# Chunked attention with a gated convolution on one core: the first half pair in two halves, fp32 value products at the start, three more half pairs with row sums on ScalarE, a new order

## The chip, the cores and the metric

The kernel runs on one core of one Trainium2 chip. Its engines are TensorE (PE; its weight loads are listed as PEld), VectorE (DVE), ScalarE (ACT), GpSimd (POOL) and SyncE (SP), which issues the DMAs. Each works off its own instructions in order. The metric is the time of the program on the device in microseconds; less is better.

## The reference

```
scores = q_c @ k_c^T / 8            # chunks of 64 rows, head size 64
attn   = exp(scores - max); attn = attn / (sum(attn) + 1e-9)
x      = attn @ v_c, heads side by side            # [8, 576, 512]
gate   = sigmoid(sum over 5 taps of conv_w[k] * x shifted by 4-k rows)
out    = (gate * (x @ w_val)) @ w_out
```

q, k and v are [8 batches, 8 heads, 576 rows, 64], all float32. The two weight matrices and the taps reach the device in 64-bit floats and are turned into float32 there.

## The kernel before, in words

The 4608 rows are cut into 9 groups g of 512 rows; the 512 columns into 4 blocks of 128. A group's attention runs in two half pairs p = 0, 1 of four heads each, which give column blocks 0, 1 and 2, 3 of x. All work is written as small pieces, and the text ORDER lists the pieces one after another; each engine gets its instructions in that order and never passes one. SLOTS says which buffer each new tile takes.

The pieces of one half pair (g, p): `lq`, `lk`, `lv` load 512 KB each. `S g p b` makes the scores of one half b (16 small fp32 matmuls) in the tile `s`, of which there is one for all half pairs. `mx` takes the row maxima (DVE), `sb` subtracts them into an `e_row` buffer (DVE), `ex` is the exponential (ACT), `sm` the row sums and their reciprocals (DVE), `nm` the division (POOL, `nmD` on DVE). For four half pairs `ng`, `ea`, `rc` stand in for `sb`, `ex`, `sm`: ACT reads the scores out of `s`, adds the negative maximum, and adds up each row as it goes, in 16 instructions. Half pair (0, 1) subtracts its maxima by four matmuls (`mh`, `mlD`, `sp`, `ep`). `T` transposes the result (8 matmuls into tile `et`), `ec` copies it (ACT), `A` multiplies by the values into two `ps` tiles (32 small matmuls). `xc` copies these into x; `xr` and `xd` split x into a rounded part and a rest for the value product.

The pieces of one group: `hl` is the halo of x, `k0` and `k g c 1..4` the five taps of block c (DVE but for `k0`), `sg` the sigmoid (ACT). `V g m c` is the value product, block c into output block m: three matmuls with w_hi x_hi, w_lo x_hi and w_hi x_lo, so that rounded operands reach nearly fp32. `vc` (ACT) or `vcD` (DVE) copies its result, `gs` (DVE) or `gsG` (POOL) multiplies it by the gate, `gr` (ACT) rounds, `gd` (POOL) or `gdD` (DVE) takes the rest. `P g t c` is the output product, three matmuls again; `oc` or `ocD` copies it and `st` stores it.

The weights: `lw` loads a block, `w1` to `w5`, `w7` turn it into float32 bits (`wq`), `w6` and `wb` split them into `v_hi`, `v_lo` (or `o_hi`, `o_lo`). `W n` issues n matmuls on a tile of zeros whose result is not used. `ps` has four tiles, all of 128x512.

In the profile nearly every row says L160 (L162 in the changed kernel), the line of the helper that records all pieces, so pieces are told apart by tiles. The tiles named t2 and t4 and a digit are shared homes; the views write most of them as t.

Of the kernel before, what the change touches and what calls it, by code (L numbers as in the profile page):

```python
# [8 lines left out]
F32 = mybir.dt.float32  # L9
# [11 lines left out]
T 0 0,ep 0 1,w4 v 0,ec 0 0,sm 0 1,w7G v 0,S 1 0 0,S 1 0 1,A 0 0,lv 0 1,w6 v 0,mx 1 0,nm 0 1,lk 2 0,lc,W 2,xr 0 0 0,
lv 1 0,sb 1 0,xc 0 0 1,xr 0 0 1,wb v 0,T 0 1,xd 0 0 0,ex 1 0,xd 0 0 1,S 1 1 0,w1G v 3,ec 0 1,S 1 1 1,sm 1 0,w7G v 1,
V 0 3 0,lq 2 1,w5 v 3,lw o 0,w2 v 3,mx 1 1,A 0 1,lk 2 1,nm 1 0,xc 0 0 0,lw o 1,lw o 3,V 0 2 0,sb 1 1,xr 0 1 0,lk 3 0,
w6 v 1,T 1 0,xr 0 1 1,w3 v 3,wbD v 1,xc 0 1 0,S 2 0 0,xc 0 1 1,w4 v 3,S 2 0 1,w6 v 2,xd 0 1 0,w7G v 3,ec 1 0,V 0 3 1,
# [12 lines left out]
V 2 1 0,w4 o 1,sg 0 1,V 2 0 3,k 1 2 1,w6 o 3,k0 2 0,V 2 1 1,gdD 0 0,vc 2 0,w7 o 1,V 2 3 2,gr 0 3,k 1 0 2,V 2 1 2,
k0 1 1,k 1 2 2,V 2 2 0,gr 0 2,gdD 0 3,w6 o 1,V 2 1 3,w3 o 2,w2 o 2,ng 4 0,P 0 1 0,gs 0 1,vc 2 1,k 1 2 3,V 2 2 1,gr 0 1,
wbD o 1,V 2 3 3,gdD 0 1,V 2 2 2,w4 o 2,ex 3 1,P 0 2 0,k 1 3 1,V 2 2 3,vc 2 3,w7 o 2,T 3 0,gdD 0 2,w6 o 2,sm 3 1,vc 2 2,
P 0 1 1,wb o 2,ea 4 0,P 0 3 0,wbD o 3,P 0 0 0,k 1 1 1,P 0 0 1,nmD 3 1,P 0 1 2,P 0 1 3,k 1 3 2,P 0 0 2,k 1 1 2,P 0 0 3,  # L40
ec 3 0,k 1 0 3,P 0 2 1,k 1 1 3,oc 0 1,P 0 3 1,k 1 0 4,k0 2 1,P 0 2 2,oc 0 0,k0D 2 2,k 1 1 4,T 3 1,k 2 2 1,P 0 3 2,
# [530 lines left out]
```

## Time and profile before

| what | value |
|---|---|
| three runs | 284.43, 286.24, 287.78 us (median 286.24) |
| span of the profiled execution, first to last instruction | 286.4 us |
| busy PE, DVE, ACT, POOL | 274.4, 245.8, 198.1, 105.2 us |
| mean granted clock of TensorE | 0.994 |
| moved by DMA | 42.47 MB |

The profiled execution is not timed apart from its span, which lies 0.2 us above the median of the three runs; the runs spread by 3.3 us. A busy time counts an engine's own instructions; PE's includes the warm-up matmuls `W`. Instructions of one engine overlap at their ends, so the distance between two starts, not the length of one, says how fast a queue moves.

### The profile page before, as it was taken

The numbers are of one execution on the slowest core, as the hardware profiler recorded it, in microseconds if no ns is written. First come the engines' busy times: TensorE is split into PE (matmuls) and PEld (weight loads), VectorE is DVE, ScalarE is ACT, GpSimd is POOL, SyncE is SP. The second block draws the span as 40 slices with busy tenths as digits, with TensorE's granted clock in tenths as the row PEclk, the third lists the DMA queues.
The fourth block names the chain that finished last, engine by engine and source line by source line (L and its number), as shares of the span: only waits on it lengthen the run. The fifth ranks groups of instructions, "written<-read, shape, count | busy, mean of one in ns | idle before, by whom it ended". The sixth has DMA issues, their size and how long they took to land.

```text
span 286.4 us, 7971 instructions
## 1 busy us (share of the span) xinstructions
PE 274.4 (96%) x3344; PEld 217.3 (76%) x3347; DVE 245.8 (86%) x357; ACT 198.1 (69%) x451; POOL 105.2 (37%) x93
## 2 busy tenths in 40 slices
PE   7978899999999999999999999989999999999994
PEld 3456688878888887878787888767678778888883
DVE  0899779999999999999999999999999899974210
ACT  2479588898999979964898696788586742751101
POOL 1457775273013506551874003976400400013100
PEclk9999799999999999999999999999999999999999
DMA  7999964457002605666250256441100121021245
GB/s 280 416 391 359 380 239 130 169 181 260 3 2 78 222 0 185 221 223 211 86 185 2 73 201 218 173 144 44 39 0 1 39 89 61 0 100 49 110 171 195
DMA packets 14291, 42.47 MB, mean 148 GB/s; under 512 B 1712, under 2 KB 1712, under 8 KB 14256
## 3 DMA queue, kind: packets, MB, share of 16 engines
q1 hardware_dynamic: 14256, 41.97, 40.9%
q8 instruction: 26, 0.43, 0.6%
q14 instruction: 9, 0.07, 0.1%
HBM read 32.53 MB, written 9.44 MB: 147 GB/s over the span
## 4 chain that ended last, share of the span: by engine, by line
PE 69%; DVE 19%; DMA 3%; issue 3%; POOL 2%; ACT 2%; SPq 0%; POOLq 0%
PE ps L160 61%; DVE acc L160 8%; PE s L160 5%; DVE t L160 4%; PE et L160 4%; DVE rs L160 3%; DMA ld<-in_v 2%; DMA ld<-in_q 1%; POOL acc L160 1%; POOL t L160 1%; DVE mx L160 1%; ACT x L160 1%; DVE t2o L160 1%; DVE t4a L160 0%; DVE x L160 0%
## 5 line engine op out<-in xcount | busy, mean ns | idle before, releaser
L160 DVE SCALAR_TENSOR_TENSOR acc<-x,cw,acc 128x516 f32<-128x516 f32 (+1 forms) x144 | 105.1, 771 | 0.9 <-POOL acc L160 0.6
L160 PE MATMUL ps<-t,v_hi 128*128 128x512 f32 x240 | 85.3, 402 | 0.0
L160 PE MATMUL ps<-t,v_lo 128*128 128x512 f32 x136 | 53.9, 396 | 0.0
L160 PEld LDWEIGHTS ps<-t,v_hi 128*128 128x128 f32 x240 | 45.2, 188 | 11.0 <-issue 0.5
L160 PE MATMUL ps<-o_hi,t 128*128 128x512 f32 x120 | 46.4, 403 | 0.8 <-ACT x L160 0.7
L160 PE MATMUL ps<-o_lo,t 128*128 128x512 f32 x76 | 30.0, 395 | 0.0
L160 DVE TENSOR_REDUCE mx<-s 128x16 f32<-128x1024 f32 x18 | 21.8, 1211 | 9.3 <-PE s L160 9.2
L160 PEld LDWEIGHTS ps<-t,v_lo 128*128 128x128 f32 x136 | 25.7, 189 | 5.1
L160 PEld LDWEIGHTS ps<-o_hi,t 128*128 128x128 f32 x120 | 22.5, 188 | 7.3 <-ACT x L160 1.1
L160 POOL TENSOR_TENSOR t<-e_row,rs 128x1024 f32<-128x1024 f32 x13 | 26.4, 2033 | 4.2 <-DVE rs L160 3.4
L160 PEld LDWEIGHTS s<-ld,ld 64*64 64x64 f32 x1152 | 19.4, 139 | 9.6 <-issue 7.7
L160 ACT CAST t<-ps 128x512 fp32r<-128x512 f32 x34 | 19.4, 596 | 10.0 <-PE ps L160 8.1
L160 PE MATMUL s<-ld,ld 64*64 64x64 f32 x1152 | 22.0, 227 | 2.9 <-issue 1.9
L160 ACT ACTIVATE e_row<-s,mx 128x64 f32<-128x64 f32 x64 | 19.0, 352 | 4.7 <-DVE mx L160 4.7
L160 POOL COPY x<-x 128x16 f32<-128x16 f32 x8 | 2.8, 354 | 52.6 <-DVE acc L160 44.9
L160 PEld LDWEIGHTS ps<-t,ld 64*64 64x64 f32 x960 | 16.3, 140 | 5.0 <-issue 2.1
L160 PE MATMUL ps<-t,ld 64*64 64x64 f32 x960 | 18.1, 225 | 1.9 <-DVE t2i L160 1.1
L160 POOL TENSOR_SCALAR acc<-x,cw 128x516 f32<-128x516 f32 (+1 forms) x7 | 12.7, 1820 | 19.2 <-ACT x L160 7.4
L160 ACT ACTIVATE acc<-x,cw 128x516 f32<-128x516 f32 (+1 forms) x24 | 17.6, 740 | 1.9 <-DVE x L160 1.8
L160 ACT ACT_TABLE_LOAD x14 | 18.0, 1283 | 0.9 <-PEq L561 0.7
L160 DVE TENSOR_REDUCE rs<-e_row 128x16 f32<-128x1040 f32 x14 | 17.2, 1228 | 1.6 <-ACT e_row L160 1.6
L160 ACT COPY x<-ps 128x512 f32<-128x512 f32 (+3 forms) x38 | 16.0, 476 | 3.3 <-issue 2.0
(302 smaller groups left out, 572.5 us busy)
## 6 DMA issues: line engine op xcount, KB each, us to landing
ld<-in_k SPq DMA_DIRECT2D x18, 512.0 KB, 5.8
ld<-in_q SPq DMA_DIRECT2D x18, 512.0 KB, 5.9
ld<-in_v SPq DMA_DIRECT2D x18, 512.0 KB, 5.0
out<-t SPq DMA_DIRECT2D x10, 256.0 KB, 2.3
acc<-in_moe_w_val SPq DMA_DIRECT2D x4, 512.0 KB, 7.5
acc<-in_moe_w_out SPq DMA_DIRECT2D x4, 512.0 KB, 7.1
out<-t2j SPq DMA_DIRECT2D x3, 256.0 KB, 2.5
out<-t2b SPq DMA_DIRECT2D x3, 256.0 KB, 3.1
```

Of the source, the lines that this page charges most:

```text
L160: return tc.keep_in_program_order(fn(*args, **kwargs))
```

## The change

Half pair (0, 0) is loaded, scored, normalised, transposed and multiplied in two halves. Its half b = 1 has its scores in the bank of `et`. Its x is no longer split: a new piece `F 0 m c` multiplies x blocks 0 and 1 as fp32 by the unsplit weights `wq`, one fp32 matmul for the three of `V`, eight pieces in all; `xr` and `xd` of (0, 0) are gone. `ea` becomes four pieces `ey g p 0..3` of four rows each, which may stand apart, and the half pairs (1, 1), (2, 1) and (4, 1) join (3, 0), (4, 0), (7, 0) and (8, 0) in that form. All `ocD` become `oc`. `gs` on DVE falls from 18 to 4 and `gsG` rises from 14 to 28; `gdD` falls from 21 to 12 and `gd` rises from 15 to 24. The warm-up matmuls fall from 31 (8, 15, 6, 2) to 21 (1, 6, 1, 1, 1, 8, 1, 1, 1). ORDER and SLOTS are written anew.

```diff
-ORDER = """zw,lk 0 0,zi,lq 0 0,W 8,lw v 2,lw v 0,lq 0 1,zr 1,zm,lk 0 1,lw v 1,zr 0,lv 0 0,lq 1 0,S 0 0 0,S 0 0 1,W 15,mx 0 0,
...
+ORDER = """zw,zi,zr 0,zr 1,lk 0 0 0,lq 0 0 0,lk 0 0 1,zm,W 1,lq 0 0 1,S 0 0 1,mx 0 0 1,sb 0 0 1,lw v 3,ex 0 0 1,w1G v 3,S 0 0 0,
+mx 0 0 0,W 6,lw v 0,lq 0 1,w3 v 0,W 1,sb 0 0 0,sm 0 0 1,lk 0 1,S 0 1 0,S 0 1 1,w2G v 3,w3 v 3,w5 v 0,ex 0 0 0,sm 0 0 0,
...
-BY_HALF = set()
+BY_HALF = {(0, 0)}
...
-        if b == 0:
-            s_ps[g, p] = tile_of("s", [P, 2, 2, 4, D], F32, banks)
-        at = s_ps[g, p]
-        if b == 1 and (g, p) in BY_HALF:
-            at = s_ps[g, p, 1] = tile_of("et", [P, 2, 2, 4, D], F32, banks)
+        alone = (g, p) in BY_HALF
+        if b == 0 or alone:
+            s_ps[g, p, b] = tile_of("et" if b else "s", [P, 2, 2, 4, D], F32, banks)
+        at = s_ps[g, p, b if alone else 0]
...
-    def sm(g, p):
-
-        rss[g, p] = r = tile_of("rs", [P, 16], F32)
-        run(V.tensor_reduce, out=r, in_=probs[g, p], op=ALU.add, axis=AX.X)
+    def sm(g, p, b=None):
+
+        if (g, p) not in rss:
+            rss[g, p] = tile_of("rs", [P, 16], F32)
+        r, e = rss[g, p], probs[g, p]
+        if b is not None:
+            r, e = r.rearrange("p (h b c) -> p h b c", h=2, b=2)[:, :, b], half_rows(e, b)
...
+    def ey(g, p, i):
+
+        if (g, p) not in probs:
+            probs[g, p] = e_rows[next(e_slot)]
+            rss[g, p] = tile_of("rs", [P, 16], F32)
+        h, b = i // 2, i % 2
+        at = half_scores(g, p, b)
+        for c in range(4):
+            j = 4 * i + c
+            run(S.activation, out=probs[g, p][:, j, 0:D], in_=at[:, h, c], func=AF.Exp, bias=mxs[g, p][:, j:j + 1],
+                scale=SCALE, accum_out=rss[g, p][:, j:j + 1])
+
     def ea(g, p):
-
-        probs[g, p] = e_rows[next(e_slot)]
-        rss[g, p] = r = tile_of("rs", [P, 16], F32)
-        sb, m = flat(s_ps[g, p]), mxs[g, p]
-        for j in range(16):
-            run(S.activation, out=probs[g, p][:, j, 0:D], in_=sb[:, j], func=AF.Exp, bias=m[:, j:j + 1], scale=SCALE,
-                accum_out=r[:, j:j + 1])
-
-    def rc(g, p):
...
-    def nm(g, p, on=G):
-        normed[g, p] = tile_of("en", [P, 16, D], F32)
-        run(on.tensor_tensor, out=normed[g, p], in0=probs[g, p][:, :, 0:D], in1=wide(rss[g, p]), op=ALU.mult)
+    def nm(g, p, *half):
+        *b, on = half if half and not isinstance(half[-1], int) else (*half, G)
+        if (g, p) not in normed:
+            normed[g, p] = tile_of("en", [P, 16, D], F32)
+        out, e, r = normed[g, p], probs[g, p][:, :, 0:D], wide(rss[g, p])
+        if b:
+            out, e = half_rows(out, *b), half_rows(e, *b)
+            r = rss[g, p].rearrange("p (h b c) -> p h b c", h=2, b=2)[:, :, b[0]].unsqueeze(3).broadcast_to([P, 2, 4, D])
+        run(on.tensor_tensor, out=out, in0=e, in1=r, op=ALU.mult)
...
+    def tr(g, p, b=None):
+        if (g, p) not in et_ps:
+            et_ps[g, p] = tile_of("et", [P, 8, P], F32, banks)
         for j in range(8):
-            run(E.transpose, out=et_ps[g, p][:, j, :], in_=normed[g, p][:, 2 * j:2 * j + 2, :].rearrange("p b k -> p (b k)"), identity=ident)
-
-    def ec(g, p, copy=S.copy):
-
...
+    def av(g, p, only=None):
         et, vv = probs_t[g, p], vt[g, p]
         for u in range(2):
-            x_ps[g, p, u] = tile_of("ps", [P, 2, 2, 2, D], F32, banks)
-        for b in range(2):
+            if (g, p, u) not in x_ps:
+                x_ps[g, p, u] = tile_of("ps", [P, 2, 2, 2, D], F32, banks)
...
+    def vf(g, m, c):
+        if c == 0:
+            v_ps[g, m] = tile_of("ps", [P, T], F32, banks)
+        run(E.matmul, v_ps[g, m], lhsT=wq["v", c].bitcast(F32)[:, m * P:(m + 1) * P], rhs=xs[g][:, c, begin(g):],
+            start=c == 0, stop=c == NH - 1)
```

PE, from the transposes of half pair (0, 1) to the first value products; first the kernel before, then the changed one (`et` are transposes, `s` scores, `ps` the value product):

```order
L160 MATMUL et_356<-ident,t_339 128x128 x8
L160 MATMUL s_369<-ld_161,ld_226 64x64 x32
L160 MATMUL ps_410<-t_348,v_hi 128x512
L160 MATMUL ps_410<-t_348,v_lo 128x512
L160 MATMUL ps_410<-t4a,v_hi 128x512
```

```order
L162 MATMUL s_319<-ld_291,ld_293 64x64 x32
L162 MATMUL et_355<-ident,t_309 128x128 x8
L162 MATMUL ps_371<-x_246,t_141 128x512
L162 MATMUL ps_371<-x_246,t2a 128x512
L162 MATMUL ps_382<-x_246,t_141 128x512
```

Before, scores of half pair (1, 1) and products of split x (three for each block) follow; now the scores come first and the products read x itself, one for each block, from two unsplit weight tiles.

ACT, from the last weight block of `v` to the first work on half pair (1, 1) in the changed kernel, and the same stretch of the kernel before (`mx` is the row maximum, `acc` on the right a raw weight):

```order
L160 CAST v_hi<-t_486 128x512
L160 ACTIVATE cw_r<-raw_cw 128x20
L160 ACTIVATE cw_t<-cw_t 128x20
L160 ACTIVATE e_row_65<-e_row_65 128x16x64
L160 ACTIVATE t_596<-acc_418 128x512
L160 CAST t_601<-ps_550 128x2x256
L160 ACTIVATE e_row_64<-e_row_64 128x16x64
L160 COPY t_621<-ps_466 128x512
```

```order
L162 CAST t_424<-ps_390 128x2x256
L162 ACTIVATE acc_437<-x_246,cw 128x512
L162 ACTIVATE acc_445<-x_246,cw 128x512
L162 ACTIVATE t2f<-acc_364 128x512
L162 ACTIVATE e_row_65,rs_486<-s_450,mx_483 128x64 x16
L162 COPY t_555<-et_529 128x1024
L162 COPY t2i<-ps_504 128x512
L162 ACTIVATE t2j<-acc_598 128x512
```

Before, two whole exponentials over `e_row` stand here; now 16 exponentials that read `s` itself stand in one piece, behind two taps and a weight step and ahead of the copy of the next transpose.

DVE, around the row maxima of half pair (7, 1), before and then changed:

```order
L160 TENSOR_REDUCE mx_2673<-s_2600 128x16
L160 SCALAR_TENSOR_TENSOR acc_2315<-x_2127,cw,acc_2315 128x516
L160 TENSOR_TENSOR t2p<-t2o,t2i 128x512
L160 TENSOR_TENSOR t_2706<-ps_2635,t_2697 128x2x256
L160 COPY x_2564<-ps_2635 128x2x256
L160 SCALAR_TENSOR_TENSOR acc_2338<-x_2127,cw,acc_2338 128x516
L160 TENSOR_TENSOR t_2706<-ps_2636,t_2697 128x2x256
L160 TENSOR_TENSOR e_row_64<-s_2600,mx_2673 128x16x64
L160 TENSOR_TENSOR t2k<-t_2633,t2j 128x512
```

```order
L162 TENSOR_TENSOR t_2572<-ps_2516,t_2550 128x2x256
L162 TENSOR_REDUCE mx_2604<-s_2482 128x16
L162 TENSOR_TENSOR e_row_65<-s_2482,mx_2604 128x16x64
L162 SCALAR_TENSOR_TENSOR acc_2243<-x_2201,cw,acc_2243 128x516 x2
L162 TENSOR_TENSOR t_2664<-ps_2615,t4a 128x2x256
L162 SCALAR_TENSOR_TENSOR acc_2380<-x_2201,cw,acc_2380 128x516
L162 TENSOR_TENSOR t_2664<-ps_2614,t4a 128x2x256
L162 SCALAR_TENSOR_TENSOR acc_2380<-x_2201,cw,acc_2380 128x516
L162 SCALAR_TENSOR_TENSOR acc_2691<-x_2587,cw,acc_2691 128x516
```

The gate product (t2p) and the rest (t2k) that stood between the taps and the splits are no longer on DVE here.

## Rows read from the trace of the kernel before

**Rows 1.** The start in stretches, and two stretches later on, by window (columns as headed).

```profile
core 0: us, PE busy (x) PEld busy (x) DVE busy (x) ACT busy (x) POOL busy (x), PEclk, DMA share, GB/s
0.00:10.00 10.00, 7.90 (x78) 3.83 (x80) 2.72 (x4) 2.85 (x4) 2.12 (x11) 1.00 0.83 318
10.00:20.00 10.00, 9.09 (x219) 5.98 (x220) 9.11 (x15) 6.24 (x10) 4.06 (x4) 1.00 1.03 410
20.00:30.00 10.00, 7.34 (x189) 5.45 (x192) 9.41 (x15) 9.47 (x16) 7.87 (x7) 1.00 0.99 362
180.00:190.00 10.00, 8.99 (x100) 7.10 (x98) 9.33 (x11) 6.59 (x10) 9.25 (x9) 1.00 0.25 95
200.00:210.00 10.00, 9.33 (x60) 7.33 (x51) 9.97 (x16) 5.01 (x16) 3.96 (x3) 1.00 0.08 28
```

**Rows 2.** Waits of PE, longest in total first.

```profile
PE s L160 <- issue: 1.9, 1, 1.9
...
PE ps L160 <- DVE t2i L160: 1.1, 1, 1.1
PE ps L160 <- DMA ld<-in_v: 0.8, 1, 0.8
```

**Rows 3.** The granted clock (PEclk) in two windows, columns as in group 1.

```profile
28.00:30.00 2.00, 0.24 (x14) 0.24 (x18) 1.58 (x5) 1.82 (x3) 1.80 (x2) 1.00 1.03 401
31.00:35.00 4.00, 4.00 (x71) 3.03 (x70) 3.96 (x7) 1.06 (x3) 2.25 (x2) 0.57 1.01 367
```

**Rows 4.** Timeline of PE from 0 to 13 us.

```profile
1.17 3.59 PE L160 MATMUL ps<-warm 128*128 128x512 bf16 x8 [1.17 <-DVE warm L160]
5.47 1.99 PE L160 MATMUL s<-ld,ld 64*64 64x64 f32 x64 [0.71 <-DMA ld<-in_q]
...
8.22 4.14 PE L160 MATMUL ps<-warm 128*128 128x512 bf16 x13 [0.22 <-issue]
```

**Rows 5.** Page, costliest groups of PE, the warm-up matmuls.

```profile
L160 PE MATMUL ps<-warm 128*128 128x512 bf16 x28 | 10.1, 509 | 1.6 <-DVE warm L160 1.2 <-issue 0.4
```

**Rows 6.** Timeline at the end of the span.

```profile
282.39 0.39 PE L160 MATMUL ps<-o_hi,t2h 128*128 128x512 f32 x1
282.82 0.58 ACT L160 COPY t<-ps 128x512 f32<-128x512 f32 x1 [0.76 <-PE ps L160]
```

**Rows 7.** Timeline of PE, value product, score and transpose.

```profile
50.24 0.40 PE L160 MATMUL ps<-t4b,v_hi 128*128 128x512 f32 x1
50.47 0.40 PE L160 MATMUL ps<-t,v_hi 128*128 128x512 f32 x1
...
58.24 1.16 PE L160 MATMUL s<-ld,ld 64*64 64x64 f32 x64
...
60.27 1.09 PE L160 MATMUL et<-ident,t 128*128 128x128 f32 x8
```

**Rows 8.** Timeline of the first half pairs, three engines.

```profile
7.52 1.23 DVE L160 TENSOR_REDUCE mx<-s 128x16 f32<-128x1024 f32 x1 [6.41 <-PE s L160]
...
17.57 1.01 ACT L160 COPY t4b<-et 128x1024 f32<-128x1024 f32 x1 [0.34 <-PE et L160]
...
19.11 1.90 POOL L160 TENSOR_TENSOR t<-e_row,rs 128x1024 f32<-128x1024 f32 x1
```

**Rows 9.** Timeline of ACT, copies and the first row-sum exponential.

```profile
47.34 0.59 ACT L160 COPY t2j<-ps 128x512 f32<-128x512 f32 x1
47.82 0.61 ACT L160 CAST t<-ps 128x512 fp32r<-128x512 f32 x1
...
51.81 0.32 ACT L160 ACTIVATE e_row<-s,mx 128x64 f32<-128x64 f32 x1 [0.93 <-DVE mx L160]
...
56.57 0.67 ACT L160 COPY t2i<-ps 128x512 f32<-128x512 f32 x1
```

**Rows 10.** Timeline of DVE and POOL side by side.

```profile
184.38 1.29 POOL L160 TENSOR_TENSOR t<-t,t 128x512 f32<-128x512 f32 x1
...
184.44 1.78 DVE L160 SCALAR_TENSOR_TENSOR acc<-x,cw,acc 128x516 f32<-128x516 f32 x1 [0.64 <-POOL acc L160]
```

More of the change, by code (lines that the diff above doesn't have):

```diff
@@ L37 @@
[L37 to L41, printed above, removed]
@@ L293, in mx @@
         if b is None:
-            run(V.tensor_reduce, out=mxs[g, p], in_=flat(s_ps[g, p]), op=ALU.max, axis=AX.X)
+            run(V.tensor_reduce, out=mxs[g, p], in_=flat(s_ps[g, p, 0]), op=ALU.max, axis=AX.X)
         else:
@@ L302, in sb @@
         if b is None:
-            run(V.tensor_tensor, out=e, in0=flat(s_ps[g, p]), in1=wide(mxs[g, p]), op=ALU.subtract)
+            run(V.tensor_tensor, out=e, in0=flat(s_ps[g, p, 0]), in1=wide(mxs[g, p]), op=ALU.subtract)
         else:
@@ L353, in rc @@
-    def rc(g, p):
+    def ey(g, p, i):
[8 more added lines that the diff above has]
+                scale=SCALE, accum_out=rss[g, p][:, j:j + 1])
+    def ea(g, p):
+        for i in range(4):
+            ey(g, p, i)
@@ L367, in ec @@
-    def ec(g, p, copy=S.copy):
-        probs_t[g, p] = tile_of("eb", [P, 2, 2, 2, P], F32)
-        run(copy, out=probs_t[g, p].rearrange("p h b a q -> p (h b a) q"), in_=et_ps[g, p])
-    def av(g, p):
+    def nm(g, p, *half):
[7 more added lines that the diff above has]
+        run(on.tensor_tensor, out=out, in0=e, in1=r, op=ALU.mult)
@@ new lines, in tr, with ec @@
+    def tr(g, p, b=None):
+        if (g, p) not in et_ps:
+            et_ps[g, p] = tile_of("et", [P, 8, P], F32, banks)
+        for j in range(8):
+            if b is not None and j // 2 % 2 != b:
+                continue
+            at = j if b is None else 4 * b + 2 * (j // 4) + j % 2
+            run(E.transpose, out=et_ps[g, p][:, at, :], in_=normed[g, p][:, 2 * j:2 * j + 2, :].rearrange("p b k -> p (b k)"), identity=ident)
+    def ec(g, p, *half):
+        *b, copy = half if half and not isinstance(half[-1], int) else (*half, S.copy)
+        if (g, p) not in probs_t:
+            probs_t[g, p] = tile_of("eb", [P, 2, 2, 2, P], F32)
+        if b:
+            run(copy, out=probs_t[g, p][:, :, b[0]],
+                in_=et_ps[g, p][:, 4 * b[0]:4 * b[0] + 4].rearrange("p (h a) q -> p h a q", h=2))
+        else:
+            run(copy, out=probs_t[g, p].rearrange("p h b a q -> p (h b a) q"), in_=et_ps[g, p])
@@ L373, in av @@
+    def av(g, p, only=None):
         et, vv = probs_t[g, p], vt[g, p]
         for u in range(2):
-            x_ps[g, p, u] = tile_of("ps", [P, 2, 2, 2, D], F32, banks)
-        for b in range(2):
+            if (g, p, u) not in x_ps:
+                x_ps[g, p, u] = tile_of("ps", [P, 2, 2, 2, D], F32, banks)
+        for b in range(2) if only is None else [only]:
             for a in range(2):
@@ L399, in xc @@
             if lo < hi:
-                run(copy, out=xs[g][:, 2 * p:2 * p + 2, col + lo - t:col + hi - t],
+                run(copy, out=x_of(g)[:, 2 * p:2 * p + 2, col + lo - t:col + hi - t],
                     in_=x_ps[g, p, u].rearrange("p b a w t -> p b (a w t)")[:, :, lo - u * half:hi - u * half])
@@ L406, in xr @@
     def xr(g, p, u):
-        if u == 0:
+        if (g, p) not in xh:
             xh[g, p] = tile_of("xh", [P, 2, T], F32R)
```

202 lines of the change are left out of this document (107 added, 95 removed).

## Prediction

> **What bounds the kernel now.** I read the windows first. After the first 30 us PE is busy nearly without a break; in the first 30 us it is busy for 7.90, 9.09 and 7.34 of each 10 us [rows 1], so 5.7 us are idle. A busy share says nothing of what the work is, so I looked at what PE does there: the warm-up matmuls, whose result nobody uses, take 10.1 us by their group [rows 5]. Next the clock: from 31 to 35 us it is granted at 0.57 of full speed, most of it at the lower of the two levels (1.2 and 2.4 GHz), behind a stretch in which PE was busy for 0.24 of 2 us [rows 3]; four microseconds at 0.57 give away 1.7 us. The first score pair takes 1.99 us and a later one 1.16 [rows 4, 7], another 0.8 us. Then the waits of PE behind the start: 0.8 us for a load of v, 1.1 us for a DVE copy, and 0.7 us in the window from 200 us, in which DVE is busy for 9.97 of 10 [rows 1, 2]. Last the end: the last matmul starts at 282.39 us, ACT copies its result from 282.82 us, and the store ends the span at 286.4, so 3.6 us lie behind PE [rows 6]. Together 5.7 + 10.1 + 1.7 + 0.8 + 2.6 + 3.6 = 24.5 us are not work of PE, and 261.9 us are. PE is the bound; what can be won is those 24.5 us, above all the 18.3 at the start. DVE is the second bound from 40 us on and makes the later waits.
>
> **The change, part by part.** I price by starts, since instructions of one engine overlap at their ends. A matmul of 128x512 takes 0.23 us (50.24 to 50.47) [rows 7], so `V` takes 0.70. A score pair takes 1.1 us, a transpose 0.9 to 1.1 [rows 7].
>
> *The fp32 product.* The trace has no fp32 matmul of 512 columns. From below, two passes at the pace of a rounded matmul are 0.47 us; from above, eight transposes of 128 fp32 columns in 1.09 us are 1.06 ns a column and, with two passes, 1.09 us for 512. I take 0.87, from the transposes at 0.85 ns a column without the tail of the last one, as scores and transposes are the nearest fp32 rows. Against 0.70 for the three matmuls of `V` the eight pieces cost 8 x 0.17 = 1.4 us more on PE (1.8 us less to 3.1 us more). The work becomes 263.3 us. The Trainium skill (FP8 and Floating Point Precision, TensorE Precision Notes) says that true fp32 takes four passes through the array; four times 0.23 us would be 0.92, and the sum would rise by 0.4 us. No run shows such a matmul yet.
>
> *What leaves the other engines.* `xr` and `xd` of (0, 0) go, and the first product needs neither `v_hi` nor `v_lo`. Three half pairs lose `sb` and `sm` on DVE, and 11 `ocD`, 14 `gs`, 9 `gdD` go to ACT and POOL: some 3 x 2.6 + 2 x 0.6 + 11 x 0.6 + 23 x 0.7, about 32 us less on DVE, where an instruction of 512 takes 0.6 to 0.7 and one of 1024 takes 1.23 [rows 8]. ACT gains 3 x 4.76 us for the row sums (51.81 to 56.57 for 16 rows of four pieces) and 11 copies of 0.5 us (47.34 to 47.82), and loses three exponentials of 1 us, two roundings and three weight steps, which leaves about 15 us more [rows 9]. POOL gains 23 products of 1.3 us, about 30 us [rows 10]. With 198 us on ACT and 105 on POOL before, neither becomes the bound over the whole span. So it is decided in the first 110 us, where all three follow PE closely.
>
> *The start.* I walked the new order of the four engines with the durations of the rows. Loads land as now: data comes in at 318 GB/s in the first 10 us, 410 in the next, 362 in the third [rows 1], so a load of 512 KB takes 1.3 us. The four half loads land at 5.4 us, the fifth and sixth load (second half pair) at 11.0, v at 14.9, q of (1, 0) at 17.4, q of (1, 1) at 24.2. Half b = 1 is scored to 6.4 us, the other half to 7.4. The DVE passes over half a tile take 0.65 us, half of 1.23 [rows 8], and sum up to both reciprocals at 10.3 and 11.5 us; here a weight step waits for its load at 8.5 us with both `sb` and `sm` queued behind it. POOL divides in two passes of 1.05 us, half of 1.9 to 2.0 [rows 8], behind two weight steps, to 14.2 us; the transposes end at 14.7, against a copy of the whole transpose at 17.57 now [rows 8]. ACT copies the two halves at 15.3 and 17.2 us, as the exponential of (0, 1) stands between them; the second half of `A` ends at 17.8. ACT then has weight steps queued between the two copies of x, which end at 19.2 and 20.8. PE meanwhile does S (1, 0) and the transposes of (0, 1), to 20.9, and begins the fp32 products then. Three of those, `A` of (0, 1), the fourth, S (1, 1), two more, five `V` and a transpose follow. ACT reaches the new row sums of (1, 1) at 28.95 us, when the maximum is ready, and ends them at 33.7. The next scores (2, 0) need the one tile `s` and so that end; PE is through with the work ahead of them at 33.8. The cover is exact, and each microsecond that ACT loses earlier comes out on PE.
>
> By 33.8 us PE will have done 4.4 us of scores, 2.75 of transposes, 2.2 of `A`, 0.9 of maxima, 5.2 of fp32 products, 3.5 of `V`: 18.95. So 14.9 us are lost at the start, against 18.3 now.
>
> *The sum.* Work 263.3, lost at the start 14.9, end 3.6. A walk of this kind leaves out handing over between engines (0.05 to 0.1 us each) and a clock that falls: 1.0 us. Later waits: DVE's share falls, but up to 110 us ACT is nearly as full as PE; 1.0 us instead of 2.6. That gives **283.8 us**, 0.9% under 286.24. I take the profile's span as the time before.
>
> **The rivals.** *A cold start.* The order has one warm-up matmul ahead of the first scores instead of eight, then seven, not fifteen. Now the eight take 3.59 us, 0.45 each, twice the warm pace, and the first scores are slow too; only late among the next thirteen (4.14 us) does the pace reach 0.2 [rows 4]. The changed order has idle stretches before and behind the second scores. If PE stays at the lower level up to the first products, the steps of the walk on its path grow: second scores 1.1 us, maxima 0.9, eight warm-up matmuls 1.7, `A` 1.1. Those are 4.8 us, all ahead of ACT's copies of x and so of the row sums on which (2, 0) waits: 288.6, slower than now. It decides from 2.4 us on; below that the kernel stays ahead. Against it: the scores and seven matmuls from 5.4 to 10.4 us are as dense a stretch as the one behind which the pace rose now.
>
> *Loads set the start.* DMA moves 362 to 410 GB/s from 10 to 30 us [rows 1] and PE waits 1.9 us at a score whose load is late [rows 2]. Half loads in rows of 2 KB, or a later fifth load, of 2 us would move every step by 2 us: 285.8.
>
> *POOL holds DVE up.* A tap (two inputs from SBUF) that starts beside a POOL product takes 1.78 us instead of 0.7 and ends with it [rows 10]. The Trainium skill (GPSIMD Engine Reference, Specifications) says that POOL's SBUF interfaces are shared with VectorE, with contention where DVE has two SBUF inputs; by that rule, which this row agrees with, all 23 moved products would speak against the change. Counted in the order up to `P 2`, only some 5 of them lie in the first 110 us, where DVE follows closely; with 1.1 us each, and half of it hidden, that is 2.7 us: 286.5. Behind that the same count leaves DVE 10 to 40 us behind PE's work.
>
> *Nothing of what I added happens.* Without the two allowances and with fp32 products at 0.75 us it is 283.8 - 2.0 - 1.0 = 280.8.
>
> **How the numbers follow.** Forecast (282.3 to 285.3) 0.36, cold start 0.14, loads 0.16, POOL 0.10, all allowances unneeded 0.24. A measurement of this kernel tells about 1% from no change: under 283.4 is faster, over 289.1 slower. Half of the forecast's case and nearly all of the last one are faster: 0.43. Slower is the cold case's upper part, with the fp32 product at its upper bound: 0.12. The rest, 0.45, is the same. The range reaches from the last case, 280.3, to between POOL's and the cold case, 287.8, and leaves out 2 in 10.
>
> **What the profile will show.** Right: fp32 products of two matmuls each from about 21 us, at 0.87 us a piece; scores (2, 0) at about 34 us, released by ACT; 15 us of PE lost before; DVE near 215 us busy, ACT near 214; no PE waits of over 0.5 us behind 110 us. Wrong: a lower granted clock or 0.43 us per matmul behind 11 us (cold start); PE or DVE waiting for loads of q or k (loads); taps of over 1.2 us in number between 40 and 110 us (POOL); the row sums of (1, 1) begun much later than 29 us, which would make the start worth nothing.

## The result, and the profile after

The changed kernel takes 288.96 us (median of four runs, 288.70 to 289.96); the kernel before, beside it, takes 287.01 (four runs, 284.43 to 290.70). The ratio is 1.0107, interval 1.0059 to 1.0155: about 1% slower, where 0.9% faster was forecast. The ratio is over fast runs alone, so without the 290.70, which lies over 1.5% above the fastest run of the same kernel. A second series of the same kernel gave 288.85 us and 1.0078 (1.0047 to 1.0109).

The profiled execution was the longest of its four runs, 289.96 us with a span of 288.2. From its page, the busy times and the group of the taps (busy us, mean ns of one, idle before):

```profile
PE 270.7 (94%) x3329; PEld 213.8 (74%) x3329; DVE 239.0 (83%) x325; ACT 213.5 (74%) x552; POOL 151.1 (52%) x120
...
L162 DVE SCALAR_TENSOR_TENSOR acc<-x,cw,acc 128x516 f32<-128x516 f32 (+1 forms) x144 | 123.2, 891 | 1.5 <-ACT acc L162 0.3
```

PE is busy for 270.7 us, of which the 21 warm-up matmuls are 7.6 by their group. The rest, 263.1 us, is the work, and 263.3 was forecast. DVE is at 239.0, not 215: the 144 taps alone take 123.2 us, against 105.1 before.

The windows that answer to [rows 1], with two further on:

```profile
core 0: us, PE busy (x) PEld busy (x) DVE busy (x) ACT busy (x) POOL busy (x), PEclk, DMA share, GB/s
0.00:10.00 10.00, 2.62 (x66) 2.02 (x67) 1.06 (x3) 1.59 (x2) 1.48 (x10) 1.00 0.78 284
10.00:20.00 10.00, 9.45 (x145) 5.00 (x149) 9.80 (x18) 5.51 (x10) 8.70 (x8) 1.00 0.93 365
20.00:30.00 10.00, 8.31 (x235) 5.42 (x224) 9.79 (x14) 8.72 (x18) 7.32 (x6) 1.00 1.01 388
30.00:40.00 10.00, 8.06 (x94) 5.38 (x94) 9.90 (x19) 8.62 (x40) 3.94 (x3) 1.00 0.57 188
...
90.00:100.00 10.00, 9.61 (x138) 7.97 (x136) 9.97 (x19) 9.82 (x22) 7.75 (x6) 1.00 0.70 238
...
120.00:130.00 10.00, 8.94 (x194) 7.22 (x197) 9.83 (x13) 6.04 (x10) 6.85 (x5) 1.00 0.30 107
```

In the first 30 us PE is busy for 20.4, where it was 24.3 in [rows 1], and for 8.06 of the next ten. DVE is 98 to 99% busy from 10 to 40 us. The waits of PE, as in [rows 2]:

```profile
PE et L162 <- DMA ld<-in_q: 6.2, 1, 6.2
PE et L162 <- DVE t L162: 2.4, 2, 1.3
PE ps L162 <- DVE t L162: 1.9, 1, 1.9
```

What waits for DVE (t is the rest of x of half pair (0, 1) or a division, x a copy) stands in the place of the loads and copies of before. The timeline of PE shows where:

```profile
7.99 1.13 PE L162 MATMUL et<-ld,ld 64*64 64x64 f32 x32 [6.22 <-DMA ld<-in_q]
...
20.19 1.11 PE L162 MATMUL s<-ld,ld 64*64 64x64 f32 x64
22.60 1.09 PE L162 MATMUL et<-ident,t 128*128 128x128 f32 x8 [1.30 <-DVE t L162]
23.55 1.10 PE L162 MATMUL ps<-x,t 128*128 128x512 f32 x2
24.49 1.02 PE L162 MATMUL ps<-x,t2a 128*128 128x512 f32 x2
25.35 1.02 PE L162 MATMUL ps<-x,t 128*128 128x512 f32 x2
26.30 1.16 PE L162 MATMUL ps<-t,ld 64*64 64x64 f32 x64
...
31.53 1.12 PE L162 MATMUL ps<-x,t 128*128 128x512 f32 x2 [1.92 <-DVE t L162]
...
38.68 1.16 PE L162 MATMUL s<-ld,ld 64*64 64x64 f32 x64
```

The scores begin at 7.99 us, released by the load of q; the walk had 5.4. The fp32 products begin at 23.55, and follow one another at 0.94, 0.86 and 0.95 us. The fifth waits 1.92 us for DVE: it needs a `ps` tile, and the subtraction `xd` of (0, 1) has to read that tile first. From there PE works with one more wait, of 0.33 us, and scores (2, 0) begin at 38.68, not 33.8. With the 18.95 us of work that lie ahead of them, 19.7 us are lost at the start: 14.9 were forecast, and the kernel before lost 18.3. The last matmul ends at 284.5 us, 3.7 us before the end (3.6 before, [rows 6]). Of 288.2 - 263.1 = 25.1 us that are not work, 1.7 remain for later waits (those in the trace are 0.39, 0.49 and 1.06, at 96, 117 and 123 us). So the start cost 4.8 us more than forecast. The other terms and the allowance of 1.0 us for handing over and the clock take a little off that: span and forecast are 4.4 us apart (288.2 for 283.8).

The miss at the start has two parts, each visible. The first scores are 2.6 us late. From them to the first fp32 product it takes 15.6 us, as in the walk (20.9 - 5.4 = 15.5). From that product to ACT's row sums of (1, 1) it takes 10.2 us instead of 8.05. The timeline of three engines in this stretch:

```profile
23.00 1.27 POOL L162 TENSOR_TENSOR t<-t,t 128x512 uint32<-128x512 uint32 x1 [1.54 <-ACT v_hi L162]
23.07 1.24 DVE L162 TENSOR_SCALAR cw_t<-raw_cw 128x20 f32<-128x20 f32 x1
...
27.59 1.37 POOL L162 TENSOR_TENSOR v_lo<-t,v_hi 128x512 fp32r<-128x512 f32 x1
...
27.76 1.24 DVE L162 TENSOR_SCALAR cw_h<-raw_cw 128x20 uint32<-128x20 uint32 x1
...
30.85 1.22 DVE L162 TENSOR_TENSOR t<-ps,t 128x512 fp32r<-128x512 f32 x2
31.99 1.22 DVE L162 TENSOR_REDUCE mx<-s 128x16 f32<-128x1024 f32 x1
...
33.77 0.31 ACT L162 ACTIVATE e_row<-s,mx 128x64 f32<-128x64 f32 x1 [1.38 <-DVE mx L162]
```

`cw_t` and `cw_h` are the conv weights, 20 values to a partition; they take 1.24 us each, and end 0.04 us after POOL's instruction beside them (23.00 + 1.27, 27.59 + 1.37). Two things hang on this queue. The subtraction (30.85) releases the fifth product, and with it all of PE's work up to scores (2, 0). The maximum of (1, 1) ends at 33.21, and ACT, which has waited for it, begins at 33.77; its row sums hold the tile `s`, and the last of them ends at 38.6 us. The two chains end within 0.1 us of each other.

### The profile page after: what moved, and what is told of

Same layout as the page of the kernel before. It is cut to its first block, busy times and chain, and to the rows that moved or that the text cites. A ratio compares the mean times of both kernels' runs of the same rounds, so it can differ in the third digit from the quotient of the medians.

```text
span 288.2 us, 8029 instructions
## 1 busy us (share of the span) xinstructions
PE 270.7 (94%) x3329; PEld 213.8 (74%) x3329; DVE 239.0 (83%) x325; ACT 213.5 (74%) x552; POOL 151.1 (52%) x120
## 4 chain that ended last, share of the span: by engine, by line
PE 63%; DVE 26%; ACT 7%; DMA 2%; issue 1%; SPq 0%; ACTq 0%; DVEq 0%
PE ps L162 55%; DVE acc L162 8%; DVE t L162 7%; PE et L162 4%; DVE mx L162 4%; PE s L162 4%; ACT e_row L162 4%; DVE rs L162 2%; DMA ld<-in_q 2%; DVE e_row L162 1%; ACT t L162 1%; ACT L162 1%; DVE x L162 1%; DVE t2a L162 1%; DVE t2q L162 1%
## 5 line engine op out<-in xcount | busy, mean ns | idle before, releaser
L162 DVE SCALAR_TENSOR_TENSOR acc<-x,cw,acc 128x516 f32<-128x516 f32 (+1 forms) x144 | 123.2, 891 | 1.5 <-ACT acc L162 0.3
L162 PE MATMUL ps<-t,v_lo 128*128 128x512 f32 x104 | 41.1, 395 | 0.3 <-DVE v_lo L162 0.3
L162 POOL TENSOR_TENSOR t<-e_row,rs 128x1024 f32<-128x1024 f32 (+1 forms) x14 | 27.0, 1933 | 22.3 <-DVE rs L162 15.9
L162 ACT ACTIVATE e_row<-s,mx 128x64 f32<-128x64 f32 x112 | 34.0, 362 | 2.4 <-DVE mx L162 2.4
L162 ACT ACTIVATION_READ_ACCUMULATOR e_row<-s,mx 128x1 f32 x112 | 28.1, 254 | 0.0
L162 DVE TENSOR_REDUCE mx<-s 128x16 f32<-128x1024 f32 (+1 forms) x18 | 21.3, 1184 | 3.9 <-PE s L162 3.9
L162 ACT COPY t<-ps 128x512 f32<-128x512 f32 x24 | 14.4, 605 | 10.3 <-PE ps L162 10.3
L162 PE MATMUL et<-ident,t 128*128 128x128 f32 x128 | 17.5, 278 | 3.3 <-DVE t L162 2.4
L162 DVE TENSOR_TENSOR t<-ps,t 128x512 fp32r<-128x512 f32 (+1 forms) x23 | 15.2, 679 | 4.9 <-PE ps L162 2.6
L162 PEld LDWEIGHTS et<-ident,t 128*128 128x128 f32 x128 | 14.0, 140 | 5.4 <-DVE t L162 2.6
```

The lines of the kernel that those rows point to most:

```text
L162: return tc.keep_in_program_order(fn(*args, **kwargs))
```

## The experiments

The theory after the result: the loads of the first half pair are late (2.6 us), and POOL's instructions lengthen DVE's queue ahead of the maximum of (1, 1) (2.2 us); PE pays both. The rivals: a cold PE, ACT's row sums holding `s`, and the products moved to POOL, which make DVE the bound later on. This table of starts is read from the timelines (us from the span's start, one execution each; times are medians of 4 to 10 runs). The clock is the lowest granted clock in a microsecond between the fifth product and scores (2, 0):

| kernel | first scores | first fp32 product F | from F to the end of the maximum of (1, 1) | clock | scores (2, 0) | time |
|---|---|---|---|---|---|---|
| changed | 7.99 | 23.55 | 9.66 | 1.00 | 38.68 | 288.96 |
| changed, again | 6.46 | 22.14 | 9.64 | 0.50 | 38.29 | 288.85 |
| e1 whole loads | 5.60 | 21.41 | 9.66 | 1.00 | 36.54 | 287.80 |
| e2 halves swapped | 4.16 | 22.44 | 9.65 | 1.00 | 37.57 | 288.41 |
| e3 warm-up | 6.88 | 22.68 | 9.66 | 0.50 | 38.76 | 289.18 |
| e4 row sums back | 6.67 | 22.21 | 9.65 | 0.50 | 38.28 | 289.81 |
| e7 conv weights early | 6.53 | 22.80 | 9.45 | 1.00 | 37.69 | 288.61 |
| e8 both | 5.51 | 21.74 | 9.43 | 1.00 | 36.62 | 288.20 |
| e9 one more | 5.68 | 22.06 | 9.80 | 1.00 | 38.16 | 289.67 |
| e10 three steps out | 5.54 | 22.31 | 10.76 | 0.50 | 39.58 | 290.36 |
| e11 POOL silent | 5.46 | 21.85 | 7.87 | 1.00 | 37.04 | 288.47 |
| e12 maximum first | 5.44 | 22.10 | 7.97 | 0.50 | 40.35 | 291.71 |

The kernel before, beside these series, took 286.06 us (e1 to e4), 285.79 (e5 to e8), 286.24 (again, e9, e10) and 286.42 (e11, e12). Where the clock fell, scores (2, 0) come about 1.0 us later: 16.15 us after F in the changed kernel, again, for 15.13 in its first execution.

**The loads.** e1 and e2:

```diff
-lk 0 0 0,lq 0 0 0,lk 0 0 1,zm,W 1,lq 0 0 1,
+lk 0 0,lq 0 0,zm,W 1,
```

> The first half pair is loaded by two loads of 512 KB again, not four of 256 KB; all else as in the changed kernel. Theory (the start is set by the loads): the first scores begin near 5.5 us, as in the kernel before, and not at 7.99; all that hangs on them moves by 2.4 us, scores (2, 0) from 38.7 to about 36.3, and the time from 288.96 to about 286.5. Rival (DVE sets the start: from 9 to 40 us it is 98% busy, and in its queue weight steps that wait for loads of w_val stand ahead of passes over the first scores): the first scores begin as early, but scores (2, 0) move by less than 0.7 us and the time stays over 288.2.

```diff
-lk 0 0 0,lq 0 0 0,lk 0 0 1,zm,W 1,lq 0 0 1,
+lk 0 0 1,lq 0 0 1,lk 0 0 0,zm,W 1,lq 0 0 0,
```

> Four half loads as in the changed kernel, but those of b = 1, which is scored first, are issued first. Theory (the loads, by the fourth that is late): scores of b = 1 begin near 5.5 us, those of b = 0 still near 8; DVE gets its first two passes, 1.3 us, done ahead of that, so scores (2, 0) move by about 1.3 us and the time to about 287.7. Rival (DVE and its weight steps): only the wait moves, and the time stays over 288.2.

e1 gave 287.80 us (five runs, 287.19 to 288.36, all under the ten of the changed kernel), ratio 1.006 (1.0039 to 1.008). The timeline of PE:

```profile
5.60 1.13 PE L162 MATMUL et<-ld,ld 64*64 64x64 f32 x32 [3.82 <-DMA ld<-in_q]
...
21.41 1.10 PE L162 MATMUL ps<-x,t 128*128 128x512 f32 x2
...
29.39 1.12 PE L162 MATMUL ps<-x,t 128*128 128x512 f32 x2 [1.93 <-DVE t L162]
...
36.54 1.16 PE L162 MATMUL s<-ld,ld 64*64 64x64 f32 x64
```

The theory holds for the start: first scores 5.60, F 2.1 us earlier, scores (2, 0) 2.1 us earlier. In time it brought 1.1 us, not 2.4. In the five other profiled executions with these half loads (the changed kernel again, e3, e4, e5, e7) the scores begin at 6.46 to 6.88 us and not at 7.99: there the loads are 1.1 to 1.5 us late, and the rest of the 2.6 us belongs to that one execution. Besides, the mean granted clock was 0.992 to 0.999 in e1's runs and 1.0 in the four of the changed kernel. Behind F nothing moved: the fifth product still waits 1.93 us. e2 got its first half at 4.16 us, its second at 6.74, and F came later than in e1: scores (0, 1), which need the fifth and sixth load, begin at 11.97 for 10.97 in e1. The time, 288.41 us (1.0081, 1.0054 to 1.0109), is over the rival's 288.2 and not the theory's 287.7; it is not clear of e1's. In both orders that were run, half loads brought F later than whole loads.

**A cold PE.**

```diff
-lk 0 0 1,zm,W 1,lq 0 0 1,
+lk 0 0 1,zm,W 8,lq 0 0 1,
```

> Eight warm-up matmuls ahead of the first scores instead of one, in the time in which PE waits for the load anyway. Cold-start rival of the prediction: the seven warm-up matmuls behind the first scores take 1.6 us instead of 3.17 and the first scores no longer than now, scores (2, 0) come 1.5 us earlier, 287.5. Theory (loads first, then DVE): PE is not what DVE and ACT wait for at the start, so nothing moves: 288.5 to 289.4, even though the seven matmuls get faster.

289.18 us (1.0101, 1.0074 to 1.0127). The first scores took 0.69 us instead of 1.13, and six of the warm-up matmuls behind them still 2.77. F comes 15.80 us after the first scores, no earlier than without them (15.56, and 15.68 in the changed kernel again); the time did not fall. The cold start was no cause.

**ACT's row sums.**

```diff
-ng 1 1,ey 1 1 1,nm 1 0,ey 1 1 0,k 0 2 1,
+sb 1 1,nm 1 0,ex 1 1,k 0 2 1,
...
-ey 1 1 2,rc 1 1,
+sm 1 1,
```

The two other pieces `ey` of (1, 1) are gone too.

> One of the three new half pairs, (1, 1), has its subtraction and its row sums on DVE again and one exponential on ACT. Theory that ACT's row sums, which hold the only score tile until 38.4 us, are what costs: scores (2, 0) begin at about 36 us, when the subtraction has released the tile, and the time falls by the 1.9 us that PE is idle from 30 to 40 us, to about 287. Rival (DVE is the bound from 9 to 190 us): 2 x 1.2 us more on DVE come out as 1.2 to 2.4 us at the end, 290 to 291.4.

289.81 us (1.0126, 1.0094 to 1.0159). The timeline of DVE and PE:

```profile
31.89 1.22 DVE L162 TENSOR_TENSOR e_row<-s,mx 128x1024 f32<-128x1024 f32 x1
...
38.28 1.16 PE L162 MATMUL s<-ld,ld 64*64 64x64 f32 x64
```

The tile `s` is free at 33.11 us, and scores (2, 0) still begin at 38.28, 16.07 us after F; in the changed kernel again, where the clock fell too, it is 16.15. So PE's own work behind the fifth product, and with it DVE's subtraction, is enough to set this start; ACT's row sums are not needed for it. DVE has 1.9 us more to do in e4, and at 42.13 us PE waits 0.86 us for a division on POOL; the new row sums of (1, 1) are worth about 1 us.

**The products on POOL.** e5 puts `gs` and `gd` of the changed kernel where they were before, e6 puts those of the kernel before where they are in the changed one; the order of the pieces stays. One line of e5, then one of e6 (35 pieces change home in either):

```diff
-gd 2 2
+gdD 2 2
...
-gs 0 1
+gsG 0 1
```

> The changed kernel with every gate product and every subtraction of a rounded half (gs, gd) on the engine that it had in the kernel before: 29 go from POOL to DVE and 6 the other way, 23 net. Theory (what leaves DVE for POOL comes back as longer taps): DVE stays at 239 us busy within 5, taps fall from 0.891 to about 0.79 us, POOL falls to about 122 us, and the time stays within 1 us of 288.96. Rival, the prediction's pricing (each product taken off DVE saved it 0.67 us): DVE rises to about 254, and since it is 98% busy from 80 to 190 us most of the 10 products there come out at the end: 292 or more.

> The kernel before with that one part of the change alone: the same 23 products (net) on POOL. Theory (longer taps): DVE stays near 246 us busy within 5, taps rise from 0.771 to about 0.87 us, and the time stays within 1 us of the kernel before. Rival (0.67 us saved each): DVE falls to about 230 us, the 2.6 us of later waits of PE shrink, and the time falls by 1.5 to 2.6 us.

e5 took 308.07 us (1.0761, 1.0688 to 1.0833), e6 294.69 (1.0292, 1.0222 to 1.0362). Of the pages, e5:

```profile
PE 276.9 (90%) x3329; PEld 216.9 (71%) x3329; DVE 251.4 (82%) x348; ACT 213.5 (70%) x552; POOL 117.4 (38%) x97
...
L158 DVE SCALAR_TENSOR_TENSOR acc<-x,cw,acc 128x516 f32<-128x516 f32 (+1 forms) x144 | 121.2, 877 | 1.4 <-ACT acc L158 0.3
```

and e6:

```profile
PE 274.7 (94%) x3347; PEld 216.8 (74%) x3347; DVE 244.1 (83%) x334; ACT 197.6 (67%) x451; POOL 139.3 (47%) x116
...
L156 DVE SCALAR_TENSOR_TENSOR acc<-x,cw,acc 128x516 f32<-128x516 f32 (+1 forms) x144 | 113.6, 833 | 2.3 <-POOL acc L156 1.5
```

Neither theory gave these times, and of the rivals only e5's "292 or more" holds, by a wide margin. e5's DVE rises by 12.4 us to 251.4, near the rival's price (0.54 for each product, not 0.67), and its taps stay long (877 ns) though POOL has 34 us less to do. e6's DVE falls by 1.7 us only, and its taps lengthen from 771 to 833 ns, as the theory says. So a product on POOL saved DVE little in the order of before, and the same product back on DVE cost it nearly its full time in the new order. The times come from waits: e5's PE waits for DVE, ACT and their copies by up to 3.7 us at a time all through the span, with PE busy for 108.2 of the last 116 us. PE's own busy time is 6.2 us longer too, at a mean granted clock of 0.983. Homes and order go together, and a product's price is not the busy time that it adds or takes away. Why the taps stay long in e5 is left open.

**POOL beside DVE at the start.** e7:

```diff
-A 0 0 0,A 0 0 1,lk 1 0,
+A 0 0 0,A 0 0 1,lc,lk 1 0,
...
-nmD 0 1,w7 v 1,lc,w5 c 0,w1 c 0,
+nmD 0 1,w1 c 0,w3 c 0,w7 v 1,w5 c 0,
...
-lk 1 1,lq 1 1,w3 c 0,
+lk 1 1,lq 1 1,
```

> The two first steps of the conv weights on DVE (128x20 values each, 1.24 us each where POOL is working) stand earlier, in a gap of POOL's work, and their load is issued two loads earlier; all else as in the changed kernel. Theory (DVE's queue, lengthened by POOL, sets the start): both take 0.2 us; the subtraction behind which the fifth fp32 product waits 1.92 us, and the maximum of (1, 1) that ACT waits for, come 2 us earlier; scores (2, 0) begin near 36.7 us instead of 38.7, and the time is 1.5 to 2 us less, near 287.2. Rival (DVE is the bound as far as 190 us for other work, and a gain at the start is given back in the waits of PE from 90 to 130 us): scores (2, 0) move, the time by less than 0.6 us.

288.61 us (ten runs, 1.0085, 1.0059 to 1.0112). The timeline of DVE and POOL:

```profile
21.70 0.17 DVE L162 TENSOR_SCALAR cw_t<-raw_cw 128x20 f32<-128x20 f32 x1
21.78 0.16 DVE L162 TENSOR_SCALAR cw_h<-raw_cw 128x20 uint32<-128x20 uint32 x1
...
22.25 1.43 POOL L162 TENSOR_TENSOR t<-t,t 128x512 uint32<-128x512 uint32 x1 [1.55 <-ACT v_hi L162]
22.46 1.76 DVE L162 SCALAR_TENSOR_TENSOR t<-t,t 128x512 uint32<-128x512 uint32 x1
...
26.91 1.38 POOL L162 TENSOR_TENSOR v_lo<-t,v_hi 128x512 fp32r<-128x512 f32 x1
...
27.07 1.25 DVE L162 SCALAR_TENSOR_TENSOR cw_h<-cw_t,cw_h 128x20 uint32<-128x20 uint32 x1
```

The two steps take 0.17 and 0.16 us in POOL's gap. But a weight step of 512 values, which took 0.68 us, now meets POOL's instruction and takes 1.76, and the next step of the conv weights takes 1.25 instead of 0.18. The hold is POOL's, and passes to a later DVE instruction; 0.2 us are won from F to the maximum. The theory's 287.2 did not come, the rival's "less than 0.6 us" did. e8 has this and whole loads.

> Whole loads for the first half pair (as in the first experiment, 287.8 us) and the conv weights' steps early. Theory (loads and DVE's queue each cost their part of the start): the gains add, scores (2, 0) near 34.6 us as the prediction's walk had them (33.8), the time near 285.8. Rival (the one hides the other): no better than 287.2.

288.20 us (ten runs, 1.0063, 1.0027 to 1.0098), as e1 within the spread. The rival holds. e9 has e8's edits and this:

```diff
-lw o 0,wb v 0,lw o 2
+lw o 0,lw o 2
...
-nm 1 0,ey 1 1 0,
+nm 1 0,wb v 0,ey 1 1 0,
```

> Whole loads, the conv weights' two steps early, and one of POOL's two subtractions between 23 and 29 us (the low part of the weights' first 128 rows, which no product needs before 44 us) moved behind the division of (1, 0); so POOL is free for about 1.5 us more of the stretch in which DVE does the maxima and subtractions that lead to the row sums of (1, 1). Theory (POOL's holds lengthen DVE's queue there; with less POOL work in the stretch they go): from the first scores to scores (2, 0) it takes 29.5 us instead of 31.1, scores (2, 0) begin near 35.0 us, and the time is about 1.5 us less than with whole loads alone, 286.3. Rival (the hold only falls on another instruction): 30.9 to 31.1 us from the first scores to scores (2, 0), and 287.6 to 288.4.

289.67 us (1.0107, 1.0071 to 1.0143), 9.80 us from F to the maximum. With one POOL instruction fewer the holds fell on two weight steps (1.75 and 1.22 us for 0.68 and 0.41). Then PE waits 1.19 us for a low part of the weights that DVE makes; ahead of it in DVE's queue stand a negation of 1.01 us and a weight step of 0.83 (0.44 and 0.56 in the changed kernel), beside the moved subtraction and a tap on POOL. The time is neither the theory's nor the rival's. e10 has whole loads, and without these three pieces:

```diff
-w2G v 3,
...
-w2G v 0,
...
-w2G v 1,
```

> Whole loads, and POOL's three multiplications of w_val by a power of two (1.5 to 1.6 us each, between 9 and 19 us) left out, so the weights are wrong by that factor. Theory (POOL's holds): DVE's three passes over two weight tiles take 0.68 us instead of 1.0 to 1.1, POOL's first division begins with the reciprocal; scores (2, 0) begin 1 us earlier than with whole loads alone, near 35.5 us, and the time is about 286.9. Rival (DVE's queue is as long without them): scores (2, 0) within 0.3 us of 36.54 and 287.4 to 288.2.

290.36 us (1.0126, 1.0094 to 1.0159). The weight steps at 14 and 17 us did get shorter (0.68 and 0.70 us), and the holds went to later ones: an addition of weight bits 1.76, a pair of limits 1.87, both conv steps 1.24 and 1.25. It is 10.76 us from F to the maximum, with three holds in the stretch where the changed kernel has two; the clock fell as well. Neither the theory's nor the rival's time came. The control, the changed kernel again beside these two:

> The changed kernel once more, unaltered, beside the next two: 288 to 289.7 us, about 1.0% above the kernel before.

288.85 us, as expected. Then POOL was silenced in the stretch altogether (e11, whole loads):

```diff
-w6 v 3,w7G v 3,
+w6 v 3,
...
-lw o 0,wb v 0,lw o 2,
+lw o 0,lw o 2,
...
-w6 v 2,w7G v 2,wb v 2,w1 o 0,
+w6 v 2,w1 o 0,
...
-nm 1 0,ey 1 1 0,
+nm 1 0,wb v 2,wb v 0,ey 1 1 0,
```

> Whole loads; of POOL's four or five instructions between 21 and 29 us the two additions to the weights' bits are left out (so the weights are wrong in their low bits) and the two subtractions stand behind the division of (1, 0), so POOL is silent in the stretch. Theory (POOL's instructions, whichever DVE instruction they meet, hold DVE up by 1.1 us each): from the first fp32 product to the end of the maximum of (1, 1) on DVE it takes 7.6 to 8.0 us, not 9.7, with no DVE instruction of 128x512 or less over 0.8 us in it. Rival (DVE's queue is that long without POOL): 9.2 us or more. The time is of less use, since the moved subtractions come late for the products behind them: 287 to 289.

```profile
21.35 0.16 DVE L162 TENSOR_SCALAR cw_t<-raw_cw 128x20 f32<-128x20 f32 x1
...
21.85 1.10 PE L162 MATMUL ps<-x,t 128*128 128x512 f32 x2
...
24.96 0.16 DVE L162 TENSOR_SCALAR cw_h<-raw_cw 128x20 uint32<-128x20 uint32 x1
...
28.51 1.21 DVE L162 TENSOR_REDUCE mx<-s 128x16 f32<-128x1024 f32 x1
...
30.64 1.85 DVE L162 SCALAR_TENSOR_TENSOR acc<-x,cw,acc 128x512 f32<-128x512 f32 x1
...
33.89 0.51 PE L162 MATMUL ps<-t,v_lo 128*128 128x512 f32 x1 [1.48 <-DVE v_lo L162]
```

7.87 us from F to the maximum, 1.79 less than with whole loads alone: the theory's number. Both conv steps take 0.16 us, and the fifth product waits for nothing. So POOL's holds are shown to make up 1.8 of the 2.2 us that the walk lacked. The time, 288.47 us (1.0068, 1.0042 to 1.0094), is no better than e1's: PE waits 0.51 us for the moved subtractions, and they hold up a tap (1.85 us) and the low part of other weights, for which PE waits 1.48 us; scores (2, 0) begin at 37.04. So the place of the 1.8 us is shown, but no run shows the time falling by as much once the holds are gone. e12 leaves POOL's work and moves the maximum ahead, with whole loads and e7's edits:

```diff
-k0 0 2,sm 1 0,xd 0 1 1,F 0 1 1,k0 0 0,xd 0 1 0,w5 o 0,S 1 1 0,S 1 1 1,mx 1 1,ng 1 1,
+k0 0 2,xd 0 1 1,F 0 1 1,k0 0 0,S 1 1 0,S 1 1 1,mx 1 1,ng 1 1,xd 0 1 0,sm 1 0,
...
-ey 1 1 0,k 0 2 1,
+ey 1 1 0,w5 o 0,k 0 2 1,
```

> Whole loads, the conv weights' two steps early, and in DVE's queue the maximum of (1, 1) and its negation ahead of the second subtraction of (0, 1) and of the row sums of (1, 0); a weight step on ACT stands behind ACT's row sums instead of ahead of them. Theory (the start hangs on the place of the maximum in DVE's queue, by ACT's row sums, which hold the score tile): the row sums begin 1.5 to 2 us earlier, scores (2, 0) near 34.9 us instead of 36.6, and the time falls to about 286.6. Rival (what is put back, the row sums and the division of (1, 0), becomes the next that is late): the transposes of (1, 0) wait for POOL by 1 us or more, and the time stays between 287.5 and 288.5.

```profile
28.86 1.21 DVE L162 TENSOR_REDUCE mx<-s 128x16 f32<-128x1024 f32 x1
...
32.45 2.21 POOL L162 TENSOR_TENSOR t<-e_row,rs 128x1024 f32<-128x1024 f32 x1 [4.88 <-DVE rs L162]
...
32.82 2.13 DVE L162 TENSOR_SCALAR t2g<-acc 128x512 uint32<-128x512 uint32 x1
...
35.60 0.50 PE L162 MATMUL ps<-t,v_lo 128*128 128x512 f32 x1 [3.00 <-DVE v_lo L162]
...
40.35 1.16 PE L162 MATMUL s<-ld,ld 64*64 64x64 f32 x64
```

291.71 us (1.0171, 1.0114 to 1.0228). The maximum ends at 30.07 us, 1.1 earlier than in e8. But the division of (1, 0) on POOL (32.45, 2.21 us) now meets a weight step of DVE, which takes 2.13 us; PE waits 3.00 us for the weights behind it, the clock falls after that wait, and scores (2, 0) begin at 40.35. The rival was right that what is put back comes late next, but it is another piece, at a higher price.

No version that was run is faster than the kernel before; the best, e1, is 0.6% behind it.

## Why the prediction was wrong

Right were: PE's work (263.1 for 263.3); the fp32 product, 0.92 us as the mean of three distances for the 0.87 taken, so 0.4 us more for eight; the end, 3.7 for 3.6; ACT at 213.5 for 214; later waits, 1.7 us for 1.0, of which the one at 122.61 us is a division on DVE beside POOL; and the walk from the first scores to the first product, 15.6 for 15.5. The Trainium skill (FP8 and Floating Point Precision, TensorE Precision Notes) says that true fp32 takes four passes through the array. Four times the 0.23 us of [rows 7] is an estimate of 0.92 us, and the three distances agree with it.

The step that failed is *the start*: 14.9 us lost were forecast, 19.7 were. Two of its terms were mis-sized. **"The four half loads land at 5.4 us"**: they land at 6.5 to 8.0. The walk took bytes and a mean rate; e1 shows that two whole loads of the same bytes land at 5.6. In the profiled execution this is 2.6 us, in the others seen 1.1 to 1.5. **"ACT reaches the new row sums of (1, 1) at 28.95 us"**: the stretch from F took 10.2 us instead of 8.05, and the two conv steps are 1.07 and 1.08 us longer than in e7 and e11, which makes 2.15 us; in e11, without POOL, 1.8 us of the stretch went. The walk priced every DVE step without POOL beside it, although the rival on POOL was in the text. "The cover is exact" was right: PE's and ACT's chains end together, and both start in DVE's queue, so each microsecond came out on PE. The executions differ in how the loss is made up. In the changed kernel again the first scores are only 1.1 us late, the stretch from F to ACT's row sums takes the same 10.2 us, and the clock, for which the walk had allowed 1.0 us together with handing over, costs 1.0 us: 19.3 us are lost at the start.

Of the rivals, the loads came true (2 us were priced; together with POOL's holds they make up the loss at the start). The row that was cited for them, 1.9 us in [rows 2], names "issue" and no load, so it was no sign of a late load. POOL did hold DVE up, but the rival looked for it in the taps from 40 to 110 us. There a tap of 128x516 takes 0.746 us in the mean, 0.745 before, and PE has one wait, of 0.39 us; the longer taps lie behind 110 us (0.963 for 0.786). It decided at 23 to 29 us, through weight steps. And a held instruction does not "end with" POOL's: in [rows 10] the tap ends at 186.22 and POOL's product at 185.67 us, so most of the tap's own time follows. The cold start, the only rival given as slower, did not occur: the eight matmuls at 17.37 us take 1.90 us in the changed kernel, and more warm-up in e3 won nothing. (The seven at 9.91 us still take 3.17 us, 0.45 each, though the granted clock of the first 10 us reads 1.00 in both kernels; that row does not show why they are slow.) The 32 us taken off DVE came out as 6.8, 18 of them lost to longer taps; where the rest went is open. As the later waits of PE came to 1.7 us for 2.6 before, no cost of that term shows here.

Before and after: the start loses 1.4 us more (19.7 for 18.3), the work is 1.2 us longer (263.1 for 261.9), the later waits 0.9 us shorter, the end the same. The sum, 1.8 us, is the difference of the two spans, 288.2 and 286.4.

## What to carry to other kernels

Walk a start with the durations that a queue has beside its neighbours, not alone: where GpSimd works through a stretch in which VectorE is full, count for a VectorE instruction that it may have to wait for the end of the GpSimd instruction that it meets (here mostly 1.1 us, 1.7 beside a division of 2.2 us), and expect that hold to move, not vanish, when one instruction is moved. Check a first load that is cut in halves against the whole one: here both orders of the halves brought the first product later. Look for two chains that end together; e4 shortened one of them and won nothing. A change of homes can't be priced by busy time apart from the order that goes with it: the same 23 products cost 9 to 19 us when moved without it.

## What the runs showed of the hardware

A DVE instruction on 20 values to a partition takes 0.16 us alone and 1.24 beside a POOL instruction, and ends 0.04 us after it. A longer one ends later by most of its own time: the weight step of 0.68 us that took 1.76 in e7 ends 0.54 us after POOL's. Those that read the scores from PSUM (1.21 us) or add up rows (1.23) take the same in both cases. The Trainium skill (SBUF — State Buffer, SBUF: two separate sides) says that the two engines share a port pair as an exclusive lock for a whole instruction, for DVE in a two-port mode or with two SBUF inputs. The trace agrees that a hold lasts to the end of POOL's instruction and that a weight step with two SBUF inputs is held. `cw_t`, with one input, is held too; whether it runs in such a mode no run here shows. The prediction had weighed two inputs alone.

The granted clock fell in some executions of the same program and not in others. The windows of PE in the profiled execution of the changed kernel:

```profile
core 0: us, PE busy (x), PEclk, DMA share, GB/s
29.00:31.00 2.00, 0.61 (x44) 1.00 0.82 289
31.00:33.00 2.00, 1.47 (x5) 1.00 0.65 231
```

and in that of the control run, the same kernel:

```profile
29.00:31.00 2.00, 0.89 (x1) 0.80 0.80 268
31.00:33.00 2.00, 2.00 (x5) 0.50 0.57 180
```

Both follow a wait of 1.92 or 1.93 us. In the second one PE runs at the lower of its two levels (1.2 and 2.4 GHz) from 31 to 33 us, the fifth product takes 1.80 us instead of 0.96, and scores (2, 0) come 1.1 us later after the first scores (31.8 for 30.7). Of the six executions in which the fifth product waits 1.92 or 1.93 us, the clock fell in four (the changed kernel again, e3, e4, e5) and not in two (its first execution, e1); in e9, after 2.05 us, it did not fall. What decides it is open.
